# An attention and two-layer expert kernel: a weights' chunk loaded in halves ahead of the constants, a planner that counts fillers singly and charges changes, and a new layout of the order

## The chip, the cores and the metric

The kernel runs on one core of one Trainium2 chip. The metric is device time in microseconds (us) of one execution, median of the runs. TensorE is called PE here (its weight loads PEld), VectorE DVE, ScalarE ACT, GpSimd POOL, SyncE SP.

## What is computed

```python
# q, k, v: (4, 8, 576, 64); w1, w2, w3: (512, 768); w_out: (768, 512)
out_d = attention(mean4(q), mean4(k), mean4(v))          # over 144 means of four
scores = where(abs(i - j) < 4, q @ k.T / 8, -1e9)        # near attention
x = repeat4(out_d) + softmax(scores) @ v                 # (2304, 512) after a transpose
h = maximum(maximum(x @ w1, x @ w2), x @ w3)
y = h @ w_out
e = argmax(y @ w_gate)                                   # 8 experts
out = gate * (relu(y @ e1[e]) @ e2[e])                   # the token's expert only
```

The weights arrive as float64 and are narrowed to float32 on the chip. Every product must be exact to about float32: each operand is split in a high part and a low part, and three products (high high, high low, low high) are summed.

## The kernel before

**Attention** is worked through in 16 units (two heads of one batch each). A unit loads q, k (`load_t`, L353), v (`load_vr`, L361) and gathered v (`load_vb`, L370). Far attention on means of four: sums of q and k, on PE as products with the identity (`add4`, L392, tile `tp`, taken by ACT at L398) or on DVE or POOL (`sum4`, L380 to L383), scores `td` (L517), maxima on DVE (L526), exponentials on ACT (L536), inverses on DVE (L495, L499), scaling (L548 on ACT, L543 elsewhere), transposes `tu` (L574), product `tz` (L585). Near attention: mask and scores `ts` (L427 to L436), maxima (L446), subtraction (L452, or on PE at L460), exponentials, transposes `tt` (L558), product `to` (L613). The far part is added by DVE (L622), or by PE from its mean (`add_far`, L632), or computed straight into `to` (`out_both`, L599). The result goes as high and low part into the blocks `xb` (L662, L664; with `x_less`, L640, the low part is made on PE). `FORMS` says for each unit which engine does which of these steps.

**Weights** of the first layer come as 18 chunks of 128x1024 words (`plan_w`, `convert`): a load into one of three buffers `raw` (L864), the magnitude on ACT (L830), four narrowing steps on DVE (L837, L839, L843, L847), the high part `wh` on ACT (L852) and the low part `wl` on DVE or POOL (L855) or over PE as `wlow` (L891, L892, taken by ACT at L896); `LOW` says where. The output weights follow in halves of that size (`plan_wo`, tile `stage`).

**Dense blocks** of 256 tokens follow the attention: `hp` (L1355), 12 products for one part of one weight, maxima on DVE (L1365), `ht` (L1372, L1376), `yp` (L1390). The first `PARTS` pieces of the first block are multiplied a quarter at a time (`plan_parts`, L1061) as its columns come. Blocks 5 to 7 use fewer products (L1264). The experts come behind.

**The order** is made by a planner (`Plan`) when the kernel is built. Every step is a job with an engine, a duration, jobs it follows, buffers it takes and gives (`get`, `put`) and a number `want`. `Plan.run` goes forward in time and takes on each engine, among the jobs that could start, the one of the smallest `want`. Engines then run their queues in that fixed order, each instruction waiting for its own inputs. Where PE would stand idle by the planner's times, it puts in fillers: products of ones (`warm`, L2489), whose result nobody reads. They are in the program for good: they run whether or not PE has something else to do. `UNITS`, `STEP`, `BEHIND`, `WEIGHTS`, `W_OUT`, `BLOCKS`, `LATER` and `ROWS` are the `want` numbers.

The constants (`cs`, with the identity) are loaded first of all (L2478), and ACT makes the copies `ident` and `nid` (minus identity) from them (L325, L327).

Of the kernel before, what the change touches and what calls it, by code (L numbers as in the profile page):

```python
# [51 lines left out]
    "dv fa pp px sk xp",  # L52
    "dv fa fn nn np pp px sq va xl xp",
    "fa fn np sk sq xl",
    "fa nn np pb sk va xp",
    "dv fn np pp sk sq va xl",
    "dv fn nb np sk",
    "fa fn nn sk xl xp",
    "fa fn nb xl",
    "dv fn va xp",  # L60
    "dv fa px sq va xl",
    "dv sk xl",
    "dv fn sq va xl xp",
    "fa fn nb sq xl",
    "fa nb np",
    "fa nn va xl xp",
    "fa va xp",
)

LOW = (  # L70
    "DVE", "DVE", "Pool", "PE", "DVE", "Pool",
    "PE", "Pool", "DVE", "PE", "PE", "DVE",
    "PE", "PE", "PE", "PE", "Pool", "DVE",
    "DVE", "Pool", "Pool", "Pool", "DVE", "DVE",
)


PARTS, PART = 6, 56838.5
UNITS = (
    19038.8, 23444.4, 33437.7, 33565.2, 37980.3, 14494.9, 18474.5, 19787.1,  # L80
    15822.2, 18490.0, 10635.2, 9464.0, 15830.1, 33419.6, 21763.8, 18489.2,
)
STEP = (
# [76 lines left out]
class Plan:  # L160
# [10 lines left out]
    def __init__(s, stock, fill=None, turns=()):  # L171
        s.fill, s.load, s.seen, s.cols = fill, 0.0, 0.0, [{} for _ in range(2)]
        s.stock = {k: [0.0] * n for k, n in stock.items()}
        s.jobs, s.free, s.port, s.turn, s.n = [], {}, 0.0, {t: [] for t in turns}, 0
# [8 lines left out]
    def add(s, eng, dur, fn, after=(), want=0.0, get=(), put=(), act=None, lat=None, port=None):  # L183
        j = dict(
            eng=eng, dur=dur, fn=fn, after=[a for a in after if a], want=want, get=get, put=put, start=None,
# [48 lines left out]
    def run(s):  # L234
# [5 lines left out]
        while any(ready.values()):  # L240
            best = None
            for e, js in ready.items():
# [16 lines left out]
                c = [x for x in c if x[0] <= t0 + (0.02)]  # L259
                if e == "PE":  # L260
# [8 lines left out]
            if j["eng"] == "PE" and s.fill and j["dur"] and s.stock["mm"]:  # L269
                free = s.free["PE"]  # L270
                if s.stock["mm"][0] <= free:
                    d = 0.216
                    n = int((t - free - (0.05 if j["want"] >= 0 else 0.4)) / d)
                    if s.busy(t) < BUSY and j["act"] < 0.8 * j["dur"] and j["want"] >= 0:
                        n = max(n, 2)
                    if n > 0:
                        end = s.pe_end(free, d * n, d * n)
                        order.append(dict(eng="PE", fn=lambda n=n: s.fill(n), start=free, dur=0, n=-1, get=(), put=()))
                        s.stock["mm"] = sorted(s.stock["mm"][1:] + [end + 0.1])
                        s.free["PE"] = end  # L280
# [3 lines left out]
            if j["eng"] == "PE" and j["dur"]:  # L284
                end = s.pe_end(t, j["dur"], j["act"])
# [23 lines left out]
class Attention:  # L309
# [12 lines left out]
    def setup(s):  # L322
        nc, P = s.nc, s.pool
        s.ident16 = P.tile([128, 128], BF16, name="ident16")
        nc.scalar.copy(out=s.ident16, in_=s.C["ident"])  # L325
        s.nid = P.tile([128, 128], F32R, name="nid")
        nc.scalar.mul(s.nid, s.C["ident"], -1.0)  # L327
        s.mask16 = P.tile([128, 3, KW], BF16, name="mask16")

    def plan_mask(s, pl, mask):  # L330
# [2289 lines left out]
```

## Time and profile before

| | us |
|---|---|
| median of 3 runs | 670.47 (669.91 to 670.55) |
| profiled execution | 670.7 |
| its span, first to last instruction | 668.8 |
| PE busy | 656.5 (98%) |
| DVE busy | 429.2 (64%) |
| ACT busy | 323.6 (48%) |
| POOL busy | 113.1 (17%) |
| mean granted PE clock | 0.994 |

Busy time is that of the hardware profiler. A busy PE need not be doing useful work: fillers count as busy, and the end of a product is modelled, so a group's time runs a little into the start of the next one. Attention and weights lie in the first 303 us; from there on the program is the same dense and expert work in both kernels.

### The profile page before, as it was taken

How to read it: one execution, taken by the hardware profiler on the slowest of the kernel's cores; microseconds unless marked ns; L12 is line 12 of the kernel's file. 1: busy time of each engine (PE TensorE's matmuls, PEld its weight loads, DVE VectorE, ACT ScalarE, POOL GpSimd, SP SyncE). 2: the span in 40 equal slices, each digit the busy share in tenths (PEclk: the TensorE clock that was granted, in tenths of full speed). 3: DMA queues.
4: the chain of work that ended last, by engine and by line, in shares of the span. 5: the costliest groups of instructions: out<-in, count | busy, mean ns of one | idle time of the engine just before them, and what ended most of it. 6: DMA issues, size and time to landing. Idle time of an engine off the chain costs nothing.

```text
span 668.8 us, 16023 instructions
## 1 busy us (share of the span) xinstructions
PE 656.5 (98%) x6272; PEld 595.4 (89%) x6272; DVE 429.2 (64%) x1070; ACT 323.6 (48%) x908; POOL 113.1 (17%) x143
## 2 busy tenths in 40 slices
PE   8899999999999999999999999999999999999995
PEld 4567799999999999999999999999998989886775
DVE  6999688998423333638535577788563563597863
ACT  4698686766422544434212223551543453347753
POOL 0314603711121010210000002103221111101011
PEclk9999999999999999999999999999999999999998
DMA  8767444543320000100000007202527453453620
GB/s 271 265 203 237 125 124 133 152 140 93 122 89 2 32 19 33 40 19 32 1 33 13 21 17 249 99 33 64 174 83 232 129 177 106 145 189 131 231 86 31
DMA packets 32245, 73.16 MB, mean 109 GB/s; under 512 B 4319, under 2 KB 4575, under 8 KB 32160
## 3 DMA queue, kind: packets, MB, share of 16 engines
q1 hardware_dynamic: 26528, 57.63, 27.1%
q0 software_dynamic: 3040, 9.70, 4.3%
q10 hardware_dynamic: 2592, 4.72, 1.9%
q8 instruction: 51, 0.84, 0.5%
q14 instruction: 34, 0.28, 0.1%
HBM read 75.18 MB, written 9.70 MB: 127 GB/s over the span
## 4 chain that ended last, share of the span: by engine, by line
PE 94%; DVE 3%; DMA 1%; issue 1%; ACT 0%; POOLq 0%; SPq 0%
PE hp L1355 33%; PE ehp L2131 12%; PE yp L1390 8%; PE eo L2103 7%; PE yp L1264 3%; PE ehp L2257 3%; PE eo L2298 3%; PE eo L2158 3%; PE racc L2420 2%; PE tz L585 2%; PE to L613 2%; PE ts L436 2%; PE hp L1061 1%; PE tt L558 1%; PE td L517 1%; PE xtp L2242 1%
## 5 line engine op out<-in xcount | busy, mean ns | idle before, releaser
L1355 PE MATMUL hp<-xb,wh 128*128 128x256 f32 x1248 | 220.0, 280 | 0.4 <-issue 0.4
L1355 PEld LDWEIGHTS hp<-xb,wh 128*128 128x128 f32 x1248 | 188.9, 188 | 1.7 <-issue 1.1
L1355 PE MATMUL hp<-xb,wl 128*128 128x256 f32 x624 | 173.2, 278 | 0.0
L1355 PEld LDWEIGHTS hp<-xb,wl 128*128 128x128 f32 x624 | 117.2, 188 | 0.0
L1365 DVE TENSOR_TENSOR hf<-hf,hp 128x256 f32<-128x256 f32 x108 | 45.2, 418 | 68.9 <-PE hp L1355 64.2
L2131 PEld LDWEIGHTS ehp<-xT,ew 128*128 128x128 f32 x672 | 78.2, 188 | 4.2 <-issue 2.5
L2131 PE MATMUL ehp<-xT,ew 128*128 128x256 f32 x672 | 80.6, 279 | 0.0
L1372 ACT CAST ht<-hf 128x256 fp32r<-128x256 f32 (+1 forms) x54 | 20.8, 388 | 72.4 <-DVE hf L1365 69.4
L2227 POOL DMA_INDIRECT xg<-y,r_go x14 | 14.7, 1052 | 173.7 <-PE hp L1355 112.5
L2315 POOL DMA_INDIRECT out_dram<-ob,r_si x17 | 17.2, 1013 | 118.3 <-ACT ob L2310 57.0
L2103 PE MATMUL eo<-eh,ehT 128*128 128x256 f32 x210 | 36.4, 280 | 0.0
L1362 ACT COPY hf<-hp 128x256 f32<-128x256 f32 x53 | 19.7, 371 | 34.4 <-PE hp L1355 34.4
L2103 PEld LDWEIGHTS eo<-eh,ehT 128*128 128x128 f32 x210 | 30.5, 188 | 2.5 <-issue 1.7
L1376 DVE TENSOR_TENSOR ht<-hf,ht 128x256 fp32r<-128x256 f32 (+1 forms) x54 | 24.4, 452 | 12.7 <-ACT ht L1372 12.4
L2103 PE MATMUL eo<-el,ehT 128*128 128x256 f32 x130 | 31.4, 276 | 0.0
L2054 ACT ACTIVATE ehT<-ehp 128x128 fp32r<-128x128 f32 (+1 forms) x40 | 13.2, 331 | 33.9 <-PE ehp L2131 33.7
L2124 DVE SCALAR_TENSOR_TENSOR ob<-eo,r_ga,ob 128x256 f32<-128x256 f32 (+1 forms) x15 | 8.6, 571 | 32.4 <-PE eo L2103 32.4
L664 POOL TENSOR_TENSOR xb<-x,xb 128x192 fp32r<-128x192 f32 (+7 forms) x32 | 16.5, 535 | 76.0 <-ACT xb L662 62.9
L1390 PE MATMUL yp<-wob,ht 128*128 128x264 f32 (+1 forms) x216 | 28.4, 285 | 0.0
L1390 PEld LDWEIGHTS yp<-wob,ht 128*128 128x128 f32 x216 | 26.8, 188 | 0.2
L1390 PE MATMUL yp<-woa,ht 128*128 128x256 f32 x216 | 26.9, 280 | 0.0
L2056 DVE SCALAR_TENSOR_TENSOR ehT<-ehp,ehT 128x128 fp32r<-128x128 f32 (+1 forms) x40 | 14.2, 354 | 18.6 <-ACT el L2039 16.5
(332 smaller groups left out, 1394.1 us busy)
## 6 DMA issues: line engine op xcount, KB each, us to landing
rw<-in_moe_w_dram SPq DMA_DIRECT2D x64, 256.0 KB
eh<-in_moe_w_dram SPq DMA_DIRECT2D x20, 512.0 KB
el<-in_moe_w_dram SPq DMA_DIRECT2D x20, 512.0 KB
raw<-in_moe_w_dram SPq DMA_DIRECT2D x18, 512.0 KB
vb<-in_vs_dram SPq DMA_DIRECT2D x16, 320.0 KB
vr<-in_v_dram SPq DMA_DIRECT2D x16, 288.0 KB
qt<-in_q_dram SPq DMA_DIRECT2D x16, 288.0 KB
kt<-in_k_dram SPq DMA_DIRECT2D x16, 288.0 KB
```

Source lines behind the costliest of these rows:

```text
L1264: s.nc.tensor.matmul(s.yb[j, k][:, 0:n], h[x], r[y], start=first and i + p == 0, stop=i == 2 and p == 2, skip_group_check=True,)
L1355: s.nc.tensor.matmul(t, s.part(a, m, g)[:, kk], s.xb[j][:, x, kk], start=n == 0, stop=n == 11)
L1362: (s.nc.scalar.copy if on == "ACT" else s.nc.vector.tensor_copy)(out=s.hf[j, m], in_=s.hp.pop((j, m, 0)))
L1365: s.nc.vector.tensor_tensor(out=s.hf[j, m], in0=s.hf[j, m], in1=s.hp.pop((j, m, g)), op=ALU.max)
L1372: s.nc.scalar.copy(out=s.ht[j][:, 0, m, c], in_=s.hf[j, m][:, c])
L1376: s.nc.vector.tensor_tensor(out=s.first_low(j) if j in SEVEN and not m else h[:, 1, m, c], in0=s.hf[j, m][:, c], in1=h[:, 0, m, c].bitcast ...
L1390: s.nc.tensor.matmul(b[j, t, g], s.ht[j][:, int(i == 1), kk, ts], s.wo(int(i == 2), kk, g)[:, 0:n], start=q == 0, stop=q == 17)
L2103: s.nc.tensor.matmul(t, x[:, c:c + 128], y, start=m == 0 and first, stop=m == 11, skip_group_check=True,)
L2131: s.nc.tensor.matmul(t, s.W1[j][a][:, f * 128:(f + 1) * 128], s.xL[:, x, j], start=n == 0, stop=n == 11,)
L2158: s.nc.tensor.matmul(s.op[k, 0], h[a][:, j, i * 128:(i + 1) * 128], s.second(b, j), start=j == 0 and w == 0, stop=j == 7 and w == 2,)
L2257: s.nc.tensor.matmul(s.hp[k][f], a[:, j], s.W1[j][b][:, f * 512:(f + 1) * 512], start=j == 0 and w == 0, stop=j == 3 and w == 2,)
L2298: s.nc.tensor.matmul(s.op[k, cols.start], a[:, j], s.second(b, j, cols), start=j == 0 and w == 0, stop=j == 7 and w == 2)
```

## The change

It has four parts.

1. One chunk of weights (`FIRST`, number 4) comes in two loads of half the size, each with its own magnitude and four narrowing steps (`convert_halves`), with a `want` of -99999. The load of `cs` and the copies `ident` and `nid` become jobs of the planner with numbers behind it, and `add4`, `sum4_v`, the weights' `wlow` and the output weights' transposes follow those two copies (`begun`).
2. The planner places fillers one by one, until less than 0.2 of the gap is left, where it sized a whole group at once.
3. It charges 0.055 when PE changes between dense products and others, and holds other jobs of PE back for a while when dense ones can run (`HOLD`).
4. All tables of numbers are new: `FORMS`, `LOW`, `PARTS` (6 becomes 2) and every `want`.

```diff
 FORMS = (
-    "dv fa pp px sk xp",
+    "fa pb pp va xp",
...
-PARTS, PART = 6, 56838.5
+FIRST, HEAD = 4, -99999.0
+PARTS, PART = 2, 58304.6
...
+TURN, HOLD = 0.055, (2.5, 0.0, 6.0, 1.5, 0.0)
...
+                if e == "PE" and s.dense and any(x[1]["dense"] for x in c):
+                    c = [x for x in c if x[1]["dense"] or not x[1]["dur"] or t0 >= x[1]["ready"] + x[1]["hold"]]
...
                     n = int((t - free - (0.05 if j["want"] >= 0 else 0.4)) / d)
+                    least = 0
                     if s.busy(t) < BUSY and j["act"] < 0.8 * j["dur"] and j["want"] >= 0:
-                        n = max(n, 2)
+                        n, least = max(n, 2), 2
                     if n > 0:
-                        end = s.pe_end(free, d * n, d * n)
+                        end, most, n = free, n, 0
+                        while n < most and (n < least or not n or end < t - 0.2):
+                            end, n = s.pe_end(end, d, d), n + 1
...
-                end = s.pe_end(t, j["dur"], j["act"])
+                end = s.pe_end(t, j["dur"] + TURN * (s.dense != j["dense"]), j["act"])
+                s.dense = j["dense"]
...
+        j = pl.add("SP", 0.25, lambda: s.nc.sync.dma_start(out=cs, in_=cst), [], HEAD + 1)
+        x = pl.add("ACT", 0.25, lambda: s.nc.scalar.copy(out=s.ident16, in_=s.C["ident"]), [j], -384.2)
+        s.begun = [x, pl.add("ACT", 0.25, lambda: s.nc.scalar.mul(s.nid, s.C["ident"], -1.0), [j], -384.2)]
...
+        for h in range(2):
+            j = pl.add("SP", 0.9, lambda h=h: load(h), js, HEAD, get=() if h else (tag + "r", tag + "t"))
+            j = pl.add("ACT", 0.34, lambda h=h: s.magnitude(*part(h)), [j], HEAD)
+            for i in range(4):
+                j = pl.add(
+                    "DVE", 0.2 if i < 2 else 0.33, lambda h=h, i=i: narrow(h, i), [j, *js], HEAD,
+                    put=(tag + "r",) if h and i == 3 else (),
+                )
...
-        nc.sync.dma_start(out=cs, in_=cst[:, n0:])
...
-        pl.free = dict(SP=2.15, PE=t, ACT=3.0, DVE=1.0, Pool=3.0)
-        at.plan_mask(pl, cst[:, off["mask"][0]:n0])
+        pl.free = dict(SP=1.5, PE=t, ACT=2.2, DVE=1.0, Pool=3.0)
+        at.plan_mask(pl, cst[:, off["mask"][0]:n0], cs, cst[:, n0:])
+        dn.begun = at.begun
```

What it does to the order is seen at two places. First SP, whose queue issues the loads, from its start; before:

```order
L2478 DMA cs<-in_consts_dram 128x130
L864 DMA raw<-in_moe_w_dram 128x1024 x3
L956 DMA wg<-in_moe_w_gate_dram 128x4x8
L361 DMA vr<-in_v_dram 96x768
L335 DMA pt<-in_consts_dram 128x192
L370 DMA vb_99<-in_vs_dram 128x640
L864 DMA raw<-in_moe_w_dram 128x1024
L353 DMA qt<-in_q_dram 128x576
L864 DMA raw<-in_moe_w_dram 128x1024
L353 DMA kt<-in_k_dram 128x576
```

and with the change (its lines are some ten higher):

```order
L874 DMA raw<-in_moe_w_dram 128x1024
L921 DMA raw<-in_moe_w_dram 128x512 x2
L339 DMA cs<-in_consts_dram 128x130
L874 DMA raw<-in_moe_w_dram 128x1024
L371 DMA vr<-in_v_dram 96x768
L998 DMA wg<-in_moe_w_gate_dram 128x4x8
L345 DMA pt<-in_consts_dram 128x192
L380 DMA vb_99<-in_vs_dram 128x640
L874 DMA raw<-in_moe_w_dram 128x1024
L363 DMA qt<-in_q_dram 128x576
L363 DMA kt<-in_k_dram 128x576
```

The constants moved behind two chunks, a whole one (number 9, whose `want` is -189695.7) and then the two halves; the first k load moved ahead of a chunk.

Second PE, behind its first fillers, of which there are 34 before and 29 now (`wlow` is the first chunk's low part, `tp` the sums of q and k, `td` far scores). Before:

```order
L2489 MATMUL warm<-const-bfloat16-1.0 128x512
L891 MATMUL wlow<-tmp,cs 128x512
L892 MATMUL wlow<-wh,nid 128x512
L392 MATMUL tp<-qt,cs 128x144 x4
L392 MATMUL tp<-kt,cs 128x144 x4
L891 MATMUL wlow<-tmp,cs 128x512
L892 MATMUL wlow<-wh,nid 128x512
L891 MATMUL wlow<-tmp,cs 128x512
L892 MATMUL wlow<-wh,nid 128x512
L517 MATMUL td<-qk 72x144 x4
```

With the change, first the low part and the fillers behind it,

```order
L2532 MATMUL warm<-const-bfloat16-1.0 128x512
L904 MATMUL wlow<-tmp,cs 128x512
L905 MATMUL wlow<-wh,nid 128x512
L2532 LDWEIGHTS const-bfloat16-1.0
L2532 MATMUL warm<-const-bfloat16-1.0 128x512
```

then, behind `tp` of q and k, the first scores and the next fillers:

```order
L439 LDWEIGHTS ident_101
L439 MATMUL ts<-mask_103,ident_101 128x256
L446 MATMUL ts<-kt,qt 58x64 x16
L446 MATMUL ts<-kt,qt 56x64 x4
L527 MATMUL td<-qk 72x144 x4
L2532 LDWEIGHTS const-bfloat16-1.0
L2532 MATMUL warm<-const-bfloat16-1.0 128x512
```

Two of three `wlow` groups and two of four `tp` groups left this stretch; 16 fillers stand between `wlow` and `tp`, 19 behind the first `td`, and 6 more behind the next near scores, ahead of the first `tu`.

## Rows read from the trace of the kernel before

**Rows 1.** the page's part 4, shares of the chain that ended last, by engine

```profile
PE 94%; DVE 3%; DMA 1%; issue 1%; ACT 0%; POOLq 0%; SPq 0%
```

**Rows 2.** busy time by stretch: PE, PEld, DVE, ACT, POOL, then PE clock, DMA

```profile
10.60:31.51 20.91, 17.56 (x114) 10.97 (x113) 19.21 (x40) 12.93 (x31) 6.83 (x5) 0.92 0.82 279
...
31.51:54.11 22.60, 21.90 (x223) 14.03 (x221) 22.31 (x56) 21.13 (x68) 4.50 (x7) 1.00 0.71 221
```

**Rows 3.** timeline to 32 us, PE: start us, us, engine, line, operation, count, idle before

```profile
0.79 9.97 PE L2489 MATMUL warm<-const-bfloat16-1.0 128*128 128x512 bf16 x34 [0.79 <-PEq L2607]
...
5.79 4.48 PEld L2489 LDWEIGHTS <-const-bfloat16-1.0 128*128 128x128 bf16 x21 [0.20 <-issue]
...
13.35 2.29 PE L392 MATMUL tp<-qt,cs 128*128 128x144 f32 x8 [1.50 <-DMA qt<-in_q_dram]
...
21.76 0.71 PE L517 MATMUL td<-qk 64*72 64x144 f32 x8
...
31.16 0.55 PE L574 MATMUL tu<-cs,ds 72*96 72x72 f32 x6 [0.29 <-DVE sm L452]
```

**Rows 4.** the same timeline, SP's first issues and ACT's first two weight operations

```profile
0.75 0.40 SPq L2478 DMA_DIRECT2D cs<-in_consts_dram  x1
...
1.20 1.37 SPq L864 DMA_DIRECT2D raw<-in_moe_w_dram  x3
...
5.46 0.66 ACT L830 ACTIVATE tmp<-raw 128x512 f32<-128x512 f32 x1 [2.21 <-DMA raw<-in_moe_w_dram]
...
6.74 0.67 ACT L830 ACTIVATE tmp<-raw 128x512 f32<-128x512 f32 x1 [0.63 <-DMA raw<-in_moe_w_dram]
```

**Rows 5.** timeline of PE, 42 to 80 us, one group of each kind

```profile
42.46 2.29 PE L392 MATMUL tp<-kt,cs 128*128 128x144 f32 x8
...
44.58 1.04 PE L891 MATMUL wlow<-tmp,cs 128*128 128x512 f32 x2
...
45.69 0.61 PE L2489 MATMUL warm<-const-bfloat16-1.0 128*128 128x512 bf16 x2
...
54.90 0.90 PE L585 MATMUL tz<-pd,vr 96*128 96x144 f32 x6
...
56.77 1.13 PE L632 MATMUL to<-dn,cs 128*128 128x288 f32 x4
...
59.32 0.78 PE L640 MATMUL to<-xb,nid 128*128 128x256 f32 x4
...
76.80 3.07 PE L599 MATMUL to<-pd,vr 96*128 96x288 f32 x12
```

**Rows 6.** timeline of PE at 97 us; chain in order of time at 302.88

```profile
96.94 0.50 PE L1355 MATMUL hp<-xb,wh 128*128 128x256 f32 x2
...
98.42 0.54 PE L574 MATMUL tu<-cs,ds 72*96 72x72 f32 x6
...
98.76 0.48 PE L1355 MATMUL hp<-xb,wh 128*128 128x256 f32 x2
...
100.32 0.71 PE L517 MATMUL td<-qk 64*72 64x144 f32 x8
...
302.88 24.49 PE hp L1355 x216
```

**Rows 7.** timeline of DVE, a far-score maximum and the last weights' narrowing

```profile
23.71 0.81 DVE L526 TENSOR_REDUCE dmx<-td 72x2 f32<-72x288 f32 x2
...
67.68 0.68 DVE L847 SCALAR_TENSOR_TENSOR tmp<-raw,tmp 128x512 int32<-128x512 int32 x1
```

**Rows 8.** DVE's groups by form to 310 us: line, names, shapes, count, busy, mean ns

```profile
L383 DVE TENSOR_REDUCE qk<-kt 128x144 f32<-128x576 f32 x8 | 5.9, 734 | 0.0
...
L446 DVE TENSOR_REDUCE smx<-ts 128x5 f32<-128x320 f32 x32 | 14.4, 483 | 4.1 <-PE ts L436 3.9
...
L837 DVE TENSOR_SCALAR tmp<-tmp 128x512 f32<-128x512 f32 x18 | 7.7, 430 | 7.4 <-ACT tmp L830 7.4
...
L837 DVE TENSOR_SCALAR stage<-stage 128x256 f32<-128x256 f32 x12 | 3.6, 303 | 3.4 <-ACT stage L830 2.9 <-ACT wob L947 0.5
```

More of the change, by code (lines that the diff above doesn't have):

```diff
@@ L173, in __init__ @@
         s.stock = {k: [0.0] * n for k, n in stock.items()}
-        s.jobs, s.free, s.port, s.turn, s.n = [], {}, 0.0, {t: [] for t in turns}, 0
+        s.jobs, s.free, s.port, s.turn, s.n, s.dense = [], {}, 0.0, {t: [] for t in turns}, 0, False
     def fork(s):
@@ L181, in fork, with add @@
         return p
-    def add(s, eng, dur, fn, after=(), want=0.0, get=(), put=(), act=None, lat=None, port=None):
+    def add(s, eng, dur, fn, after=(), want=0.0, get=(), put=(), act=None, lat=None, port=None, dense=False, hold=0.0):
         j = dict(
+            dense=dense, hold=hold,
             eng=eng, dur=dur, fn=fn, after=[a for a in after if a], want=want, get=get, put=put, start=None,
@@ L340, in plan_mask @@
         j = pl.add("SP", 0.27, load, (), -384.2, get=("pt",))
-        s.masked = pl.add("ACT", 0.25, take, [j], -384.2, put=("pt",))
+        s.masked = pl.add("ACT", 0.25, take, [j, *s.begun], -384.2, put=("pt",))
     def tile(s, tag, shape):
@@ L855, in low, with convert @@
         (s.nc.vector if on == "DVE" else s.nc.gpsimd).tensor_tensor(out=lo, in0=t, in1=hi.bitcast(F32), op=ALU.subtract)
-    def convert(s, pl, want, d, src, words, vals, hi, lo, tag, on, first=None, put=None):
+    def convert(s, pl, want, d, src, words, vals, hi, lo, tag, on, first=None, put=None, halves=False):
         st = {}
@@ L877, in low @@
             vals.append(st["v"])
-        j = pl.add("SP", d[0], load, [first], want, get=(tag + "r",))
-        j = pl.add("ACT", d[1], magnitude, [j], want, get=(tag + "t",))
-        for i in range(4):
-            j = pl.add("DVE", d[2 + i // 2], lambda i=i: narrow(i), [j], want, put=(tag + "r",) if i == 3 else ())
+        if halves:
+            j = s.convert_halves(pl, st, src, words, vals, tag)
+        else:
+            j = pl.add("SP", d[0], load, [first], want, get=(tag + "r",))
+            j = pl.add("ACT", d[1], magnitude, [j], want, get=(tag + "t",))
+            for i in range(4):
+                j = pl.add("DVE", d[2 + i // 2], lambda i=i: narrow(i), [j], want, put=(tag + "r",) if i == 3 else ())
         more = put(lambda: st["v"], j) if put else None
@@ L893, in less @@
             vals.append(st["v"])
-        j = pl.add("PE", d[5], less, [j, more], want, get=("mm",), put=(tag + "t",))
+        j = pl.add("PE", d[5], less, [j, more, *s.begun], want, get=("mm",), put=(tag + "t",))
         return pl.add("ACT", d[6], lambda: s.nc.scalar.copy(
@@ L898, in convert, with convert_halves, load, part @@
             put=("mm",))
+    def convert_halves(s, pl, st, src, words, vals, tag):
+        js = []
+        def load(h):
+            if not h:
+                st["w"], st["v"] = words.pop(0), vals.pop(0)
+            c = slice(512 * h, 512 * h + 512)
+            s.nc.sync.dma_start(out=st["w"][0].rearrange("p k f -> p (k f)")[:, c], in_=src[:, c])
+        def part(h):
+            return st["w"][1][:, 2 * h:2 * h + 2], st["v"][:, 2 * h:2 * h + 2]
+        def narrow(h, i):
+            s.narrow(*part(h), i)
+            if h and i == 3:
+                words.append(st["w"])
+        for h in range(2):
+            j = pl.add("SP", 0.9, lambda h=h: load(h), js, HEAD, get=() if h else (tag + "r", tag + "t"))
+            j = pl.add("ACT", 0.34, lambda h=h: s.magnitude(*part(h)), [j], HEAD)
+            for i in range(4):
+                j = pl.add(
+                    "DVE", 0.2 if i < 2 else 0.33, lambda h=h, i=i: narrow(h, i), [j, *js], HEAD,
+                    put=(tag + "r",) if h and i == 3 else (),
+                )
+            js = [j] if h else []
+        return j
     def plan_w(s, pl, when):
@@ L1214, in plan_out_seven @@
                 get=(("mm" if q in (1, 5) else "at"),) if new else (),
-                put=("hT",) if i in (len(PIECES) - 1, max(ends[q] for q in (1, 2, 4))) else (),
+                put=("hT",) if i in (len(PIECES) - 1, max(ends[q] for q in (1, 2, 4))) else (), dense=True,
             )
```

78 lines of the change are left out of this document (39 added, 39 removed), and 8 rows, old and new, of the table STEP.

## The prediction

> **What bounds the kernel now.** I read the shares of the chain first: 94% of it is PE's [rows 1]. So the time is PE's queue: its work, its fillers and the time in which it waits or runs slowly. Next come the stretches, to see where PE loses time. From 10.60 to 31.51 us PE is busy 17.56 of 20.91 and its granted clock is 0.92; from 31.51 to 54.11 it is busy 21.90 of 22.60 at full clock [rows 2]. In the second stretch, though, DVE is busy 22.31 of 22.60 [rows 2]: it narrows the weights, and PE is filled up with fillers around it. The reader should see two things there: the one stretch with a real loss is the first 20 us behind the opening fillers, and until about 68 us, where the last weights' narrowing starts [rows 7], DVE sets the pace for what PE may do. The timeline shows the loss itself: the first `tp` waits 1.50 for q, and the first `tu` starts at 31.16 [rows 3]. Behind 303 us the two orders have the same PE work, so the whole change is priced in front of it.
>
> **The change, part by part.** The sum is made against the profiled execution's own 670.7; that is 0.2 above the median of 670.47, so the result is lowered by as much at the end. 0.2% (1.3 us) is about what a measurement of this kernel can tell from no change.
>
> *Real work on PE.* Counted over the whole order. A group's busy time runs some 0.2 into the next group: `tp` is 2.29 long, and the next group starts 2.12 behind it [rows 5]. One unit fewer is summed on PE: two `tp` groups, 2 x 2.12 = -4.24. Two units fewer add the far mean there (`to` from `dn`, 1.13 - 0.2): -1.86. One unit fewer makes its low part there (`x_less`, 0.78 - 0.2): -0.58. One unit more computes both parts at once (`to` from `pd`, 3.07 - 0.2): +2.87; so one `tz` fewer, -0.70. One chunk more goes over `wlow`, from 44.58 to 45.69: +1.11 [rows 5]. The pieces of `PARTS` only move between two lines, at 0. Sum -3.4. What PE sheds, ACT, DVE and POOL take up; on POOL and ACT it lies beside other work, on DVE see the second rival.
>
> *Fillers.* 93 stand where 59 stood in front of 303 us: 5 fewer in the opening group, 39 more behind it. Of the opening 34 the last 21 go at 4.48 / 21 = 0.213 each, the higher of PE's two clock levels, the ones ahead of them slower [rows 3]. The five that go are of the fast ones. So 34 x 0.213 = +7.25. At 0.25 apiece, if each group of them costs a little at its ends, it is +8.4.
>
> *Waits in the first stretch.* Now PE loses 20.91 - 17.56 = 3.35 idle, and 0.08 x 17.56 = 1.4 to the clock [rows 2]: 4.75. The fillers take the place of these waits. The opening ends at 10.76 - 5 x 0.213 = 9.7; behind it come `wlow` (1.11), 16 fillers (3.4), so `tp` at 14.2, when q, which now comes at 13.35 [rows 3] with the same bytes ahead of it, is there. What is left is the wait of the first `tu`. From the first `td`'s end (21.76 + 0.71 = 22.47) to `tu` it takes 8.7 now [rows 3], of which DVE is 1.24 late with the maximum [rows 7]: the chain itself is 7.45. PE's own road there is 25 fillers, 5.33, and one group of near scores. So the wait is at most 2.1; I take 1.0, since that group covers about half of it. Change: 1.0 - 4.75 = -3.75. Bounds: -4.75 (no wait left) and 0 (as much lost as now).
>
> *Changes between dense and other products.* Two runs of twelve dense products last 98.42 - 96.94 = 1.48 and 100.32 - 98.76 = 1.56 with the change behind them; by 24.49 for 216 twelve are 1.36 [rows 6]. So a pair of changes costs 0.12 to 0.20, say 0.16. The order has 50 such pairs before, 43 after: -1.1 (bounds -0.8 and -1.4).
>
> *The loads.* Now `cs` is issued at 0.75 and the first weights at 1.20, and ACT starts on them at 5.46 [rows 4]. With the weights first all of DVE's narrowing may start 0.45 earlier; since DVE sets the pace up to 68 us, I book -0.45 (bounds 0 and -0.45). The words of the change say that the halves come first, but the order puts a whole chunk ahead of them; I count nothing for the halves. What waits instead: `nid` and the first high part stand on ACT behind `cs`, and `wlow` behind them. If `cs` lands as the second chunk does now, before 6.74 [rows 4], `nid` is made by 7.5 and the opening fillers hide it until 9.7.
>
> Sum: -3.4 + 7.25 - 3.75 - 1.1 - 0.45 = **-1.45**, or 669.25 on the profile's scale, **669.0** on that of the median, 0.2% faster.
>
> **The rivals.**
>
> *Half of it is eaten by DVE: no change.* DVE's order ahead of the last narrowing holds more rows than before: three sums of q or k at 0.734 and two maxima at 0.483 [rows 8], 3.2; the halves cost 0.7, since a step of half the size takes 0.303 where a whole one takes 0.430 [rows 8], 4 x 0.18; the other rows nearly cancel. With the overlap between rows about 3.4. Starting 0.45 earlier, the last narrowing ends 2.95 later than now (67.68 + 0.68 = 68.4 [rows 7]), at 71.3. Behind it PE has about 3.4 us less to do (up to the 84th dense product the two orders hold the same work, so nearly all that was shed lies behind it, and half of the change pairs). That is -0.45 if DVE alone sets the pace: 670.0. The Trainium skill speaks against halving as well: VectorE: DVE Perf Modes, "The TRN2 errata", says that many small tiles pay a fixed cost each, 58 cycles at 0.96 GHz in its table, or 0.24 for four more instructions; the trace has 0.7, and with the page's figure this rival would be 0.5 faster. For it: DVE's 22.31 of 22.60. Against: behind 72 us DVE has slack. Chance 0.32.
>
> *DVE stands while PE fills: slower.* DVE's queue takes its maxima in order. With the change the first one stands behind five chunks; at the present pace, 23.71 - (5.46 + 0.66) us [rows 4, 7] for seven chunks and four other rows, five are done by some 17.3. But the first `td` ends only at 14.2 + 4.24 + 1.1 + 0.65 = 20.1, because 16 fillers stand ahead of `tp`. DVE would stand for 2.8 us, and everything behind it moves: the last narrowing ends at 74.1, 5.7 later, against the 3.4 won behind it. That is +2.3: 670.5 + 2.3 = 672.8. It decides at the last narrowing's end: before 71.8 the change gains, behind 73.1 it is slower by over 0.2%. For it: fillers can't shrink when they aren't wanted. Against: the loads of the fourth to sixth chunk come late anyway and take part of the 2.8. Chance 0.22.
>
> *All fits.* No wait is left and change pairs cost 0.20: -3.4 + 7.25 - 4.75 - 1.4 - 0.45 = -2.75, 667.7. Chance 0.10.
>
> *The loads come one behind the other.* If none overlapped, each would take the first one's 5.46 - 1.20 = 4.3, `cs` would land behind 9.4, and the first `wlow` with all behind it would slip by 2 or more: 671 to 672. The second chunk's landing 1.28 behind the first [rows 4] speaks against it. By the Trainium skill (DMA: Bandwidth & Descriptors, "Anatomy of one DMA") each transfer pays about 2.0 us besides its bytes over 436 GB/s; paid in a row, `cs` would land at 11.3, and the time would be 671.3. Chance 0.03, with the second rival's sign or none.
>
> **How the numbers follow.** The forecast has 0.33 and is the likeliest case; all fits has 0.10: faster 0.43. No change: 0.32 for the first rival and 0.02 of the last. Slower: 0.22 and 0.01. The forecast's own range is 667.7 to 669.5. The range to hold 8 in 10 takes in "all fits" with more than its price (fillers that replace waits in the second stretch too, 0.7 idle there [rows 2], and as much again at dense products), 666.2, and the slower rival whole: 666.2 to 672.8.
>
> **What would show it.** Right: PE's clock at 1.00 between 10 and 30 us; the first `tp` without a wait; the first `tu` near 27.5 instead of 31.16; `cs` landed before 7.5; the last narrowing ending before 71.8. Block 5's first dense product, now at 302.88 [rows 6], would start at 301.4, and everything behind it last as long as now. Wrong: DVE idle between 17 and 20 us, the last narrowing behind 73; or PE waits of over 1 us behind `tu`, on maxima and narrowing; or a change of time behind 303 us, where I expect none.

## The result, and the profile after

The changed kernel takes 675.89 us (median of 4 runs, 674.72 to 676.99), the kernel before 670.51 beside it: 1.0083 times as long, 95% interval 1.0067 to 1.0099. The prediction was 669.0, faster; its range ended at 672.8. The profiled execution is the slowest of the four, 676.99, with a span of 675.1.

The first stretch came out as forecast. By windows (us, then busy time of PE, PEld, DVE, ACT and POOL with the number of rows, PE's granted clock, DMA share, GB/s), the third stretch of the kernel before (its first two are in [rows 2]):

```profile
54.11:89.02 34.91, 34.91 (x465) 29.15 (x464) 28.48 (x69) 25.80 (x87) 15.60 (x19) 1.00 0.53 160
```

and all three of the kernel after:

```profile
10.60:31.51 20.91, 19.63 (x175) 11.53 (x175) 20.00 (x37) 12.45 (x32) 9.53 (x10) 1.00 0.88 294
31.51:54.11 22.60, 21.48 (x177) 14.55 (x177) 19.36 (x46) 18.75 (x55) 2.61 (x3) 1.00 0.69 215
54.11:89.02 34.91, 32.28 (x424) 24.00 (x430) 29.91 (x77) 29.66 (x104) 7.70 (x11) 0.95 0.50 159
```

PE is busy 19.63 of 20.91 at full clock where it was 17.56 at 0.92 [rows 2]. Its timeline has the first `tp` at 14.34 without a wait and the first `tu` at 27.83 instead of 31.16 [rows 3], 3.3 us won:

```profile
10.82 3.67 PE L2532 MATMUL warm<-const-bfloat16-1.0 128*128 128x512 bf16 x16
14.34 2.20 PE L402 MATMUL tp<-qt,cs 128*128 128x144 f32 x8
...
27.83 0.55 PE L584 MATMUL tu<-cs,ds 72*96 72x72 f32 x6 [0.93 <-ACT ds L558]
```

From there on it is lost, and more. The second and third window show it: DVE, busy 22.31 of 22.60 before [rows 2], is busy 19.36, and PE, which didn't idle between 54 and 89 before, idles 2.6 there and falls to a clock of 0.95. Block 5's first dense product on PE before; then, after, the last step of the last weights' narrowing on DVE and the same product:

```profile
302.71 0.41 PE L1355 MATMUL hp<-xb,wh 128*128 128x256 f32 x2
```

```profile
72.76 0.68 DVE L857 SCALAR_TENSOR_TENSOR tmp<-raw,tmp 128x512 int32<-128x512 int32 x1
...
307.28 0.40 PE L1399 MATMUL hp<-xb,wh 128*128 128x256 f32 x2
```

The narrowing ends at 73.44 instead of 68.36 [rows 7], 5.1 later. Block 5 starts 4.6 later. What lies between is as long as it was: 233.84 against 234.35. PE's busy time in front of and behind the last narrowing, by windows, first before and then after:

```profile
0.00:68.36 68.36, 63.52 (x572) 40.96 (x573) 59.88 (x130) 49.27 (x135) 16.80 (x20) 0.98 0.75 239
68.36:302.71 234.35, 234.22 (x2862) 223.52 (x2862) 137.30 (x383) 122.20 (x453) 52.64 (x81) 1.00 0.27 81
```

```profile
0.00:73.44 73.44, 68.03 (x619) 42.45 (x624) 62.99 (x138) 51.27 (x143) 14.76 (x20) 0.98 0.72 229
73.44:307.28 233.84, 233.42 (x2826) 222.67 (x2825) 140.46 (x409) 127.93 (x517) 43.41 (x66) 1.00 0.26 79
```

So the whole loss in front of 303 us has come up by the last narrowing. DVE's 5.1 there are 3.1 more busy time (62.99 against 59.88) and 2.0 more idle time (10.45 against 8.48; 1.2 of the idle time is won at the start, which is now at 4.95 instead of 6.15, so 3.2 are new waits). The first narrowing step of DVE, before and after:

```profile
6.15 0.43 DVE L837 TENSOR_SCALAR tmp<-tmp 128x512 f32<-128x512 f32 x1 [6.15 <-ACT tmp L830]
```

```profile
4.95 0.43 DVE L847 TENSOR_SCALAR tmp<-tmp 128x512 f32<-128x512 f32 x1 [4.95 <-ACT tmp L840]
```

The largest of the waits is one for v. Before, on PE and SP:

```profile
33.29 1.00 PE L585 MATMUL tz<-pd,vr 96*128 96x144 f32 x6
...
34.32 0.33 SPq L361 DMA_DIRECT2D vr<-in_v_dram  x1
```

After, the timelines of SP, PE, DVE and ACT, and the chain's row:

```profile
46.17 0.33 SPq L874 DMA_DIRECT2D raw<-in_moe_w_dram  x1
46.59 0.38 SPq L371 DMA_DIRECT2D vr<-in_v_dram  x1
...
43.37 3.18 PE L609 MATMUL to<-pd,vr 96*128 96x288 f32 x12
...
46.59 6.93 DMA vr<-in_v_dram
...
53.64 0.56 DVE L413 TENSOR_TENSOR vr<-vr 96x384 f32<-96x384 f32 x1 [1.93 <-DMA vr<-in_v_dram]
...
54.62 0.80 ACT L425 ACTIVATE vr<-vr,cs 96x192 f32<-96x192 f32 x2 [1.16 <-DVE vr L414]
...
56.36 1.00 PE L595 MATMUL tz<-pd,vr 96*128 96x144 f32 x6 [2.14 <-ACT sm L480]
...
58.63 2.13 PE L642 MATMUL to<-dn,cs 128*128 128x288 f32 x4
```

Read it from the top. There is one buffer for v. Before, unit 0 read it last in `tz`, at 33.29, and the second load was issued at 34.32. Unit 0's new form (`pb`) reads it in `out_both` (L609), which ends at 46.55. So the second load, which the planner put behind a weights' chunk, is issued at 46.59; it takes 6.93 us, and DVE, whose order is fixed, stands for 1.93, ACT and PE behind it. PE's granted clock falls after its wait of 2.14: it is 0.72 from 56.36 to 58.63 and 0.50, the lower of the two levels, from there to 60.68, where four products that took 1.13 [rows 5] take 2.13.

Behind 303 us there is a second loss, 1.9 us (from block 5's first dense product to the last `eo`: 360.85 against 358.91). It comes up at one place. The routing products `inv` and the products around them, before:

```profile
460.88 2.10 PE L1706 MATMUL inv<-r_rh,r_oj 128*128 128x78 f32 x18
462.81 11.15 PE L2131 MATMUL ehp<-xT,ew 128*128 128x256 f32 x96
```

and after, with the window behind `inv`:

```profile
463.98 2.55 PE L1750 MATMUL inv<-r_rh,r_oj 128*128 128x78 f32 x18
466.36 0.70 PE L2202 MATMUL eo<-eh,ehT 128*128 128x512 f32 x2
466.90 0.57 PE L2202 MATMUL eo<-el,ehT 128*128 128x512 f32 x1
467.26 1.05 PE L2202 MATMUL eo<-eh,ehT 128*128 128x512 f32 x2
468.12 0.63 PE L2202 MATMUL eo<-el,ehT 128*128 128x512 f32 x1
468.55 11.92 PE L2175 MATMUL ehp<-xT,ew 128*128 128x256 f32 x96
...
466.36:470.55 4.19, 4.19 (x18) 3.72 (x18) 0.88 (x8) 1.38 (x2) 1.05 (x1) 0.59 0.17 26
```

The planner, which starts there from another state, put `inv` ahead of the last six `eo` products. They and the first `ehp` run at a mean clock of 0.59. What made it fall isn't shown: PE is busy without a break from 463.98 on, as it is in the kernel before.

### The profile page after: what moved, and what is told of

Its sections match the earlier page's. It is cut to its first block, busy times and chain, and to the rows that moved or that the text cites. A ratio compares the mean times of both kernels' runs of the same rounds, so it can differ in the third digit from the quotient of the medians.

```text
span 675.1 us, 16141 instructions
## 1 busy us (share of the span) xinstructions
PE 662.1 (98%) x6280; PEld 597.1 (88%) x6287; DVE 429.5 (64%) x1095; ACT 331.1 (49%) x979; POOL 101.7 (15%) x128
## 4 chain that ended last, share of the span: by engine, by line
PE 90%; DVE 5%; DMA 2%; issue 1%; POOL 1%; ACT 1%; SPq 0%; POOLq 0%; DVEq 0%
PE hp L1399 33%; PE ehp L2175 12%; PE yp L1434 8%; PE eo L2147 7%; PE yp L1307 3%; PE ehp L2301 3%; PE eo L2342 3%; PE racc L2464 2%; DMA vr<-in_v_dram 2%; PE eo L2202 2%; PE tz L595 2%; PE to L623 2%; PE ts L446 2%; PE tt L568 1%; PE td L527 1%; PE xtp L2286 1%
## 5 line engine op out<-in xcount | busy, mean ns | idle before, releaser
L1399 PE MATMUL hp<-xb,wh 128*128 128x256 f32 x1280 | 225.5, 280 | 0.4 <-issue 0.4
L1399 PEld LDWEIGHTS hp<-xb,wh 128*128 128x128 f32 x1280 | 193.7, 188 | 1.5 <-issue 1.1
L1399 PE MATMUL hp<-xb,wl 128*128 128x256 f32 x640 | 177.6, 278 | 0.0
L1399 PEld LDWEIGHTS hp<-xb,wl 128*128 128x128 f32 x640 | 120.4, 188 | 0.0
L1420 DVE TENSOR_TENSOR ht<-hf,ht 128x256 fp32r<-128x256 f32 (+1 forms) x54 | 22.4, 417 | 10.5 <-ACT ht L1416 9.9
L546 ACT ACTIVATE ds<-td,dmx 72x144 f32<-72x144 f32 x64 | 23.4, 374 | 7.2 <-DVE smx L484 3.5
```

What stands on the lines that cost most here:

```text
L546: s.nc.scalar.activation(out=st["ds"][:, a, :, h], in_=t[:, a].rearrange("p (k t) -> p t k", t=3), func=ACTF.Exp, bias=st["dm"][:, h, a:a ...
L1399: s.nc.tensor.matmul(t, s.part(a, m, g)[:, kk], s.xb[j][:, x, kk], start=n == 0, stop=n == 11)
L1420: s.nc.vector.tensor_tensor(out=s.first_low(j) if j in SEVEN and not m else h[:, 1, m, c], in0=s.hf[j, m][:, c], in1=h[:, 0, m, c].bitcast ...
```

## The experiments

All edits but one keep the order of everything they don't name; times are medians, against the kernel before of the same runs.

| run | us | before | ratio (95%) | last narrowing ends | block 5 starts | from there to the last `eo` |
|---|---|---|---|---|---|---|
| before | | | | 68.36 | 302.71 | 358.91 |
| after | 675.89 | 670.51 | 1.0083 (1.0067 to 1.0099) | 73.44 | 307.28 | 360.85 |
| v_early | 675.09 | 670.39 | 1.0068 (1.0052 to 1.0085) | 71.55 | 305.93 | 360.23 |
| whole_chunk | 675.01 | 670.39 | 1.0067 (1.0050 to 1.0084) | 72.12 | 306.07 | 360.23 |
| inv_last | 673.46 | 670.39 | 1.0049 (1.0030 to 1.0068) | 73.43 | 307.26 | 358.94 |
| old_tables | 680.99 | 670.39 | 1.0154 (1.0137 to 1.0171) | 71.87 | 311.36 | 361.97 |
| thin_sums | 674.74 (one run) | 670.55 | | 70.76 | 304.44 | 361.26 |
| few_fill | 677.25 | 670.55 | 1.0095 (1.0074 to 1.0116) | 72.33 | 308.31 | 360.23 |
| combo | 673.19 | 670.55 | 1.0041 (1.0025 to 1.0056) | 71.55 | 305.46 | 358.54 |
| combo_pe | 674.41 | 670.65 | 1.0056 (1.0043 to 1.0069) | 73.63 | 307.71 | 358.54 |
| combo_pool2 | 673.24 | 670.50 | 1.0034 (1.0020 to 1.0048) | 71.71 | 305.88 | 358.53 |
| combo_pool3 | 674.00 | 670.50 | 1.0053 (1.0036 to 1.0070) | 70.30 | 305.11 | 358.53 |
| combo_thin | 672.40 | 670.73 | 1.0031 (1.0015 to 1.0047) | 71.32 | 305.03 | 358.52 |
| before_start | 670.43 | 670.55 | 0.9997 (0.9987 to 1.0007) | 67.87 | 302.38 | 358.88 |
| before_pe | 671.03 | 670.65 | 1.0004 (0.9993 to 1.0015) | 67.60 | 302.13 | 358.88 |
| before_more | 674.29 | 670.73 | 1.0049 (1.0032 to 1.0066) | 71.66 | 306.53 | 358.88 |

The last three columns come from the profiled execution of each run; block 5's start is its first dense product. The difference of the first two of them is 233.7 to 234.9 in all runs but few_fill (236.0) and old_tables (239.5): as a rule block 5 starts some 234 us behind the last narrowing. In thin_sums and combo_thin the far scores, and so the tokens' experts, are others.

**v_early: the one buffer for v.**

```diff
+        if u == 1:
+            vr = s.st[u]["vr"] = s.stage[0:96, 0:768].rearrange("p (t r d) -> p t r d", t=3, r=4)
+        else:
             vr = s.st[u]["vr"] = s.tile("vr", [96, 3, 4, D])
...
+        order = pl.run()
+        early = at.jobs[1]["lr"]
+        order = [j for j in order if j is not early]
+        i = next(i for i, j in enumerate(order) if j is at.jobs[4]["lk"])
+        order.insert(i + 1, early)
```

> The changed kernel; only the second unit's load of v differs: it goes into the buffer that the output weights use later, so it needn't wait until the first unit's v is free, and it stands on SP ahead of four loads of weights (issued near 32 us, not at 46.59). All other instructions keep their places. Theory A (the one buffer for v, held longer by the first unit's new form, costs the time): DVE's wait of 1.93 at 53.64 and PE's wait of 2.14 at the second tz go, the last weights' narrowing ends near 71.5 instead of 73.44, PE's granted clock from 54 to 89 us is back at 1.00, block 5's first dense product starts 2 to 3 us ahead of 307.44; 673 us (672.5 to 674). Rival B (DVE simply has more rows, and something else is late at the same place): the wait goes to another row, under 1 us is won, 675 to 676.

The waits went as theory A says. The timelines of DVE and PE:

```profile
51.74 0.55 DVE L416 TENSOR_TENSOR stage<-stage 96x384 f32<-96x384 f32 x1
...
70.92 0.63 DVE L860 SCALAR_TENSOR_TENSOR tmp<-raw,tmp 128x512 int32<-128x512 int32 x1
...
55.02 1.00 PE L598 MATMUL tz<-pd,stage 96*128 96x144 f32 x6 [0.54 <-ACT sm L483]
...
305.93 0.40 PE L1402 MATMUL hp<-xb,wh 128*128 128x256 f32 x2
```

DVE doesn't wait at v's sum any more, the narrowing ends at 71.55, PE's clock is 1.00 from 54 to 89, block 5 starts 1.35 earlier. But the medians fell by 0.8 only, short of A's 673, and the intervals of the two runs overlap. In the profile the held buffer is shown as a cause; by block 5's start it is a quarter of the loss at most. The size of the wait isn't fixed: inv_last, the same program up to there, shows 1.20 in place of 1.93, with the narrowing ending at 73.43.

**whole_chunk: the halves.**

```diff
-            c = slice(512 * h, 512 * h + 512)
-            s.nc.sync.dma_start(out=st["w"][0].rearrange("p k f -> p (k f)")[:, c], in_=src[:, c])
+            if not h:
+                s.nc.sync.dma_start(out=st["w"][0].rearrange("p k f -> p (k f)"), in_=src)
...
-            return st["w"][1][:, 2 * h:2 * h + 2], st["v"][:, 2 * h:2 * h + 2]
+            return st["w"][1], st["v"]
```

(The second half's magnitude and narrowing steps are left away with it.)

> The changed kernel with chunk number 4 loaded, converted and narrowed whole at the places of its first half (one load and five instructions where ten and two stood); the order is otherwise unchanged. By the prediction's price the halves cost DVE 0.7, so 675.2 to 675.9. If the halves are what made the kernel slower, it is 674 or less. If they bring the first narrowing forward, it is slower: 676.5 and more.

0.9 won by the medians (the intervals overlap), 1.3 at the last narrowing: a little more than the price of 0.7. DVE's wait for v was 0.46 in this run, so part of it may be that. The halves bring nothing forward, since a whole chunk stands ahead of them.

**inv_last: the order behind 450 us.**

```diff
+            run = p.run()
+            i = [i for i, x in enumerate(run) if x["eng"] == "PE" and x["dur"] == 0.6][0]
+            k = [k for k, x in enumerate(run) if x["eng"] == "PE" and x["dur"] == 1.36 and k > i][0]
+            if led:
+                run.insert(i, run.pop(k))
```

> The changed kernel with one edit behind 450 us: the 18 inv products stand behind all 48 eo products, as in the kernel before, instead of ahead of the last six. Theory C (this order costs the 1.95 us that came up behind 303 us, by a low clock for the products behind inv: six eo took 2.19 there where 1.36 is usual, and the next ehp 0.24 each): 674.0 to 674.5, with the same start of the first ehp behind inv as before plus 4.2. Rival D (the clock fell there by chance of that one run): 675.5 to 676, no difference.

```profile
465.46 2.10 PE L1750 MATMUL inv<-r_rh,r_oj 128*128 128x78 f32 x18
467.39 11.15 PE L2175 MATMUL ehp<-xT,ew 128*128 128x256 f32 x96
```

Theory C, with 673.46 even below its 674.0. The rows are those of before again, and block 5 to the last `eo` takes 358.94, as before (358.91). The order ahead of six `eo` costs 1.3 us in v_early, whole_chunk and few_fill (360.23), and 1.9 and 2.4 in after and thin_sums.

**old_tables.** All tables of before in the new code (with `FIRST` and `HEAD`); here the planner lays out everything anew.

> The new code (halves ahead of the constants, fillers placed singly, changes charged, dense products held together) with the tables of the kernel before: forms, weights' engines, six pieces and all want numbers. Theory E (the new layout holds the loss, the code itself is harmless): 669 to 671. Rival F (the code's halves, fillers or holding cost it): 673 or more.

681, in rival F's range and far above it. The last narrowing ends 3.5 later than before, and behind it PE idles 5.7 up to block 5 where it idled 0.1. But the old tables were made for the old rules; the run doesn't say what the new rules cost with tables of their own, only that they don't give the old order. No run takes the filling, the charge for changes, `HOLD` or the two pieces of `PARTS` by itself.

**thin_sums: less work for DVE.**

```diff
-            nc.vector.tensor_reduce(out=o, in_=x, op=ALU.add, axis=AX.X)
+            nc.vector.tensor_copy(out=o, in_=x[:, :, 0])
```

> The changed kernel, in which DVE's sums of q or k (five ahead of the last narrowing, 0.737 each) copy the first of the four rows instead of adding all four: the far scores, and with them the expert routing, are not the reference's, so only the time up to block 5's first dense product (307.28 in the changed kernel) is read. Theory G (up to the last narrowing DVE sets the pace one for one, and PE, with the same work left behind it as before, hands it on): the rows shrink to about 0.25, five of them 2.4 us; the last narrowing ends near 71.0 instead of 73.44 and block 5 starts near 304.9. Rival H (PE's fixed fillers set the pace there): the narrowing ends earlier, block 5 stays within 0.5 of 307.28.

Theory G by its numbers: the last narrowing 2.7 earlier, block 5 2.8 earlier. But more than the sums changed: DVE's wait at v is 0.82, for PE, in place of 1.93 for the load, and DVE was busy 0.66 more in the first 10.6 us. So this profile doesn't price the rows one for one.

**few_fill: the fillers.**

```diff
+            if small:
+                nc.tensor.matmul(t[:, 0:8], one(128), one(8), start=True, stop=True)
+                return
```

with `small` for the groups between 27 and 300 us of the plan (the trace has eleven of them).

> The changed kernel with each of the ten groups of fillers behind 27 us and in front of 303 (18 products of 512 columns) cut to one product of 8 columns. Theory G (DVE sets the pace): PE only waits where it filled, the last narrowing ends as before at 73.4 and the time stays within 0.7 of 675.9; it may get worse if PE's clock falls. Rival H (fillers cost their own length): 3 us are won, near 673.

By windows:

```profile
31.51:54.11 22.60, 19.79 (x167) 14.27 (x165) 19.52 (x47) 18.46 (x56) 2.61 (x3) 0.92 0.71 216
54.11:89.02 34.91, 31.31 (x417) 23.34 (x421) 29.63 (x75) 29.13 (x104) 7.71 (x11) 0.95 0.52 156
```

PE is busy 2.7 less in the two windows than in the kernel after (51.10 against 53.76), and the time is 1.4 us longer by the medians (the intervals overlap), not 3 shorter. The last narrowing ends 1.1 earlier, but PE has more left to do then: block 5 starts 236.0 behind it, not 233.8. PE's clock is 0.92 between 31 and 54, where it was 1.00. Rival H is out: taking these fillers away doesn't win their length. How much of that is waits in their place, and how much the lower clock, the run doesn't part.

**combo: the three edits at once.**

> The changed kernel with three edits at once: the second unit's v loaded early into the output weights' buffer, the 18 inv products behind all eo products, chunk 4 whole. If the edits' gains add up (0.8, 1.3 and 0.8 by the times so far against 675.9): 673.0. If the early v and the whole chunk take away the same wait (in both, DVE's wait of 1.93 for v was gone): 673.8. It stays slower than before by 2 or more in either case, since DVE's 3.1 us of added rows ahead of the last narrowing remain.

673.19, 2.7 off the changed kernel's 675.89, near the 2.9 that the expectation added up with 1.3 for `inv` (what that order costs in v_early and whole_chunk). By the medians alone, with the 2.4 of inv_last, it would be 4.1. This is the first gain whose interval lies clear of the changed kernel's. 2.6 us against before remain.

**combo_pe and before_pe: POOL's low parts over PE.** Each low part that POOL made early becomes two products `wlow` and a copy on ACT, for fillers taken out (19 in combo_pe, 5 in before_pe). The edit in both, at the place of POOL's instruction:

```diff
+            p = st["p"] = s.bank(512, "wlow")
+            s.nc.tensor.matmul(p, s.C["ident"], st["v"], start=True, stop=False)
+            s.nc.tensor.matmul(p, s.nid, hi(), start=False, stop=True)
```

> The three edits of combo (673.19), and the four low parts of weights that POOL made between 13 and 28 us go over PE (two products and a copy on ACT, as other chunks do) in place of 19 fillers there. In combo DVE's narrowing steps beside those POOL rows took 0.66, 0.99 and 1.07 longer than usual. Theory G (DVE sets the pace one for one, and POOL's rows cost DVE this much): the last narrowing ends 2.7 earlier, at 68.9, block 5's first dense product starts at 302.8, 670.5. Rival: POOL's rows cost DVE nothing that matters, or PE's new products delay the first far scores and exponentials and DVE waits for those: 672.5 or more.

> The kernel before with the weights ahead of the constants (as in before_start, 670.43) and the first two low parts that POOL made (15.40 and 29.74 us, 1.28 each) over PE, the second in place of five fillers. Beside them DVE's steps took 1.05 and 0.38 longer. Theory G: the last narrowing ends 1.4 earlier, 669.0, which would beat both kernels. Rival: the first product delays q's and k's sums by 0.7 to 1.1 and the first far scores with them, and DVE or PE waits for that: 670 to 671.

The rival in both. In combo_pe a new product waits for a high part (1.63 at 14.94), weights' loads are issued later (the two at 10 us are out at 14.5, not 13.4), and DVE stands for the magnitudes. The first of these waits is of the loads and not of the edit (combo_thin, without it, has 1.09 at 10.72). DVE's timeline:

```profile
10.80 0.43 DVE L850 TENSOR_SCALAR tmp<-tmp 128x512 f32<-128x512 f32 x1 [1.03 <-ACT tmp L843]
15.48 0.43 DVE L850 TENSOR_SCALAR tmp<-tmp 128x512 f32<-128x512 f32 x1 [1.39 <-ACT tmp L843]
22.14 0.43 DVE L850 TENSOR_SCALAR tmp<-tmp 128x512 f32<-128x512 f32 x1 [2.79 <-ACT tmp L843]
```

**before_start: the weights first, alone.**

```diff
-        nc.sync.dma_start(out=cs, in_=cst[:, n0:])
...
+            if sp == 2 and j["eng"] == "SP" and j["dur"] == 1.8:
+                nc.sync.dma_start(out=cs, in_=cst[:, n0:])
...
+            if act == 2 and j["eng"] == "ACT" and j["dur"] == 0.55:
+                nc.scalar.copy(out=at.ident16, in_=C["ident"])
+                nc.scalar.mul(at.nid, C["ident"], -1.0)
```

> The kernel before, with one part of the change alone: two whole chunks of weights are loaded ahead of the constants, and ACT makes the two copies of the identity behind the first two magnitudes; everything else, tables and fillers included, keeps its place. Theory G (DVE sets the pace up to the last narrowing, so an earlier start is handed on whole): DVE starts at 4.9 to 5.1 instead of 6.15, the last narrowing ends 1.1 earlier, 669.3. Rival: the first q, k and v come as late as before and DVE only waits for them later, no change (670.0 to 670.7).

No change that can be measured. DVE started at 5.38, 0.8 earlier than before, and the last narrowing ended 0.5 earlier, not 1.1.

**combo_pool2 and combo_pool3: DVE's sums on POOL.** In `sum4`: `on = "Pool" if u in (3, 5) else on`, and `(1, 3, 5)`.

> Combo (673.19) with the sums of q and k of units 3 and 5 on POOL in place of DVE: three rows of 0.737 ahead of the last narrowing (31.55, 55.27 and 56.60), at a time when POOL does little. Theory G: the last narrowing ends 1.7 to 2.2 earlier (71.55 before; POOL's two rows a sum may hold DVE up by 0.2 each), 671.0 to 671.7. Rival (POOL's longer way delays the scores, or its rows cost DVE what they save): 672.8 to 673.5.

> The same with unit 1's two sums on POOL as well, five rows of 0.737. Theory G: the last narrowing ends 2.7 to 3.6 earlier, 669.8 to 670.7, the time of the kernel before or a little less. Rival: POOL is busy with the weights' low parts there, unit 1's far scores come later, and DVE waits for those: 672 or more.

Nothing won by the medians. In combo_pool2 the narrowing ends where it did: DVE, with three rows less, waits for ACT at three places between 52 and 59 (0.45, 0.27 and 0.93; combo has one there, 0.35) and loses 0.34 at 48.42 beside a row of POOL. In combo_pool3 it ends 1.25 earlier, and block 5 only 0.35.

**before_more and combo_thin: DVE's rows by themselves.** `before_more` makes the first four `near_sum` twice; `combo_thin` is combo with the edit of thin_sums.

> The kernel before, in which DVE makes the first four sums of the near exponentials twice (0.80 each, at 37.32, 46.82, 60.54 and 65.77): 2.9 us more of DVE ahead of the last narrowing, no other row changed and the same result. Theory G (DVE sets the pace there, each row is paid): the last narrowing ends near 71.3 instead of 68.36, block 5 starts near 305.6 instead of 302.71, 673.4. Rival I (DVE's waits take it up, or PE has slack behind): 670.5 to 671.5.

> Combo (673.19) with DVE's sums of q or k cut to a copy of the first of four rows (the far scores are left without the other three): 2.4 to 2.7 us less of DVE ahead of the last narrowing. Theory G: the last narrowing ends near 69.0 instead of 71.55 and the time is near 670.6, that of the kernel before; then early v, the order behind 450 us and DVE's rows are all of the loss. Rival I: a wait takes the rows' place as it did when three of them went to POOL, 672.5 or more.

before_more, on DVE and PE:

```profile
70.98 0.68 DVE L849 SCALAR_TENSOR_TENSOR tmp<-raw,tmp 128x512 int32<-128x512 int32 x1
...
306.53 0.41 PE L1357 MATMUL hp<-xb,wh 128*128 128x256 f32 x2
```

2.9 us of DVE rows, with nothing else changed, end the last narrowing 3.3 later, start block 5 3.8 later and cost 3.6 us by the medians (674.29 against 670.73). In front of 68 us DVE's rows are paid in full, and somewhat more, in the kernel before. In combo_thin the reverse gave 0.8 of the expected 2.6, within the noise. By windows up to the last narrowing, combo and then combo_thin:

```profile
0.00:71.55 71.55, 67.47 (x619) 41.32 (x624) 63.05 (x134) 50.45 (x142) 17.20 (x20) 1.00 0.74 236
```

```profile
0.00:71.32 71.32, 66.37 (x619) 41.12 (x624) 61.37 (x134) 50.45 (x142) 15.27 (x20) 1.00 0.72 237
```

DVE is busy 1.7 less and idle 1.5 more. 1.09 of that is a wait for a magnitude at 10.72, ahead of any of the sums (ACT itself waits 1.08 there for a weights' load), and 0.46 one for exponentials at 58.37. So this profiled run doesn't show the rows by themselves, and 1.7 us of the loss (672.40 against 670.73) stay open: DVE is still busy 1.5 longer than before (61.37 against 59.88) and idle as much longer (9.95 against 8.48), and no run parted the two.

No version beat the kernel before: before_start and before_pe equal it.

## Why the prediction was wrong

**The step that failed.** The sum adds up PE's time, and it put at nothing what PE waits for and loses to its clock behind the first stretch, though the text itself said that DVE sets the pace there. Up to block 5 PE's time can be added up again from the windows. Fillers are busy 24.17 where they were 16.44: +7.7 (forecast +7.25). The rest of PE's busy time, with the clock's loss taken out as the prediction did it, fell by 4.2 (forecast -3.4 and -1.1). The first stretch lost 3.35 idle and 1.4 to the clock and now loses 1.28 and nothing: -3.5 (forecast -3.75). But from 31.51 to 89.02 PE idles 3.75 where it idled 0.70, and 0.05 x 32.28 = 1.6 goes to the clock: +4.6, for which the sum has no term. Another 1.9 came up behind 303 us, where it has none either. Together that is 6.5; the two profiles differ by 6.3.

**What bounds.** The chain's 94% for PE [rows 1] were read as PE's queue being the time. But a filler counts as PE, and PE's time follows DVE's steps: before_more, with 2.9 us more of DVE and not a row more of PE, cost 3.6. A sum over PE needs a term for each wait that DVE's later steps bring, and fillers cover such a wait only where the planner foresaw it.

**Real work on PE, -3.4.** As a sum over PE the term was good. Where it lies was not: the first two rivals took it as 3.4 less to do behind the last narrowing, since both orders hold the same work up to the 84th dense product. The mark was wrong, because the narrowing ends long before that product. At its end the kernel before had done 27 dense products and the changed one 12. The windows of `hp` alone, before and then after:

```profile
0.00:68.36 68.36, 4.71 (x27) 3.59 (x27) 0.00 (x0) 0.00 (x0) 0.98 0.75 239
```

```profile
0.00:73.44 73.44, 2.72 (x12) 1.83 (x12) 0.00 (x0) 0.00 (x0) 0.98 0.72 229
```

PE's busy time behind it is 234.22 and 233.42: 0.8 less. The pieces of `PARTS` that "only move between two lines, at 0" may be part of that, as work that PE can do while DVE narrows; no run changed them alone.

**Fillers, +7.25, and waits in the first stretch, -3.75.** The waits went as forecast: the first `tu` at 27.83 (27.5 forecast), a wait of 0.93 (1.0). That won nothing: the 3.3 us won at the first `tu` are gone by the last narrowing, which ends 5.1 later. few_fill showed that nothing is won by taking out the fillers behind 27 us; no run took out those in front without other products in their place.

**DVE.** The first rival's price for DVE's rows was good: about 3.4 with the halves; measured are 3.1 more busy time. Part of that is luck: by the timelines the 128x512 narrowing steps that ran longer than their usual 0.43 and 0.69 are longer by about 3.4 in sum before and 4.5 after, all of them beside a row of POOL (last section), and the rival didn't count that. With nothing won behind the narrowing, it would have read 670.5 + 2.95, or 673.4. What it and the forecast missed are DVE's new waits, 3.2, of which v's is 1.93. Of `pb` the prediction counted the products (+2.87 on PE) and not what it holds: the one buffer for v, 12 us longer. The forecast's own mark held: "the last narrowing behind 73" was to be wrong, and slower.

**DVE stands while PE fills.** The sign was this rival's, and almost its number for the last narrowing (74.1; 73.44 measured), but not its mechanism. The first maximum, at 20.90 behind `td`, found DVE busy without a gap from 14.15 on.

**Changes between dense and other products, -1.1, and the loads, -0.45.** The first lies within PE's time behind the last narrowing, which is 0.5 shorter in all; no run parted it. The loads: DVE starts 1.2 earlier; alone on the kernel before (0.8 earlier in before_start) this gave 0.5 at the last narrowing and no measurable time. `cs` landed in time, as forecast: ACT makes `ident` and `nid` from it at 6.95 and 7.14, so the loads didn't come one behind the other. The fixed 2.0 us of the last rival stand in the Trainium skill (DMA: Bandwidth & Descriptors, "Anatomy of one DMA") for transfers issued by GpSimd; these are issued by SP, and no run here prices that fixed part.

**Behind 303 us** the prediction expected no change, since the work is the same. The order isn't: the planner goes on from another state, and one group of 18 moved ahead of six products. inv_last took back 1.9 in profile and 2.4 in the medians (673.46 against 675.89; the intervals touch).

**The halves** were priced by the trace at 0.7 and by the table of the Trainium skill (VectorE: DVE Perf Modes, "The TRN2 errata") at 0.24. whole_chunk won 0.9; the half-size steps took 0.28 and 0.41 where whole ones take 0.43 and 0.69, which is 0.55 for the chunk. The trace's price was the nearer one. The same section of the Trainium skill says that its table's 58 cycles fall short of what was measured, and gives a fixed term of about 150 cycles; four instructions would be 0.63 by that, an estimate from its figure. The rows' 0.55 agrees with it.

The loss as measured, by the medians: 2.7 for v, the halves and `inv` together (combo; about 0.8, 0.9 and 1.3 to 2.4 alone, where v and the halves are not clear of the noise), 0.8 for DVE's sums (combo_thin, not clear of it either), and 1.7 whose cause stays open.

## What to carry to other kernels

Where an engine is filled with work that nobody reads, its share of the chain doesn't say what sets the pace: find the engine whose rows end the stretch, here DVE's last narrowing, and price every term by what it does to that point and by what work is left behind it. For each step that changes its form, look up which single buffer it holds and until when; the next load waits for that, and behind it an engine in fixed order. Where the sum is made over the filled engine all the same, give the waits of every stretch a term, also of those that had none. And compare the whole order, also where the work is the same.

## What the runs showed of the hardware

A low part on POOL (a row of 1.28 us) holds up a narrowing step of DVE beside it. In the kernel after:

```profile
13.63 2.71 POOL L865 TENSOR_TENSOR wl<-tmp,wh 128x512 fp32r<-128x512 f32 x2 [1.42 <-ACT wh L862]
18.81 1.28 POOL L865 TENSOR_TENSOR wl<-tmp,wh 128x512 fp32r<-128x512 f32 x1 [2.47 <-ACT wh L862]
...
15.23 1.40 DVE L849 TENSOR_SCALAR tmp<-tmp 128x512 int32<-128x512 int32 x1
...
18.91 1.73 DVE L853 SCALAR_TENSOR_TENSOR tmp<-raw,tmp 128x512 int32<-128x512 int32 x1
```

DVE's two steps take 0.43 and 0.69 elsewhere, so they are 0.97 and 1.04 longer beside POOL's rows, more than the 0.68 that DVE needs for a low part itself. Taking the row away shows that it is the cause: in before_start a step beside POOL's first low part (14.64) takes 1.74 at 14.73, and in before_pe, without that row, the same step takes 0.69 at 15.09. DVE's maxima beside such rows kept their length (29.81 before, 0.80 for two).

DVE's start differs from run to run: in the first 10.60 us it is busy 4.78 in the kernel after and 5.44 in thin_sums, 4.86 in combo and 4.11 in combo_thin, with the same loads in front. So the last narrowing of one profile can be off by most of a microsecond, and smaller differences between two profiles carry little here. It need not be: inv_last, the same program as the kernel after up to there, is busy 4.05 in that time, and its narrowing ends at 73.43 against 73.44, because its wait for v is shorter.
